# First blocks of a fused convolution, SiLU and product kernel: new list, two rounding steps on VectorE, seven products of zeros ahead of the first block's products

## The chip, the cores and the metric

The kernel runs on one core of a Trainium2 chip. The metric is the device time of one execution in microseconds (us). Five engines work in it, each on its own instruction stream and in the order of that stream: TensorE (PE, matrix products; PEld is its weight load), VectorE (DVE), ScalarE (ACT), GpSimd (POOL) and SyncE (SP), which here only issues DMA transfers. An engine waits at an instruction whose input is not ready, and everything behind that instruction on the same engine waits with it.

## The reference

The input `x` is 8 sequences of 4096 tokens with 192 channels. Each channel is convolved along its sequence with 7 causal taps, which the 24 channels of a head share and which are a softmax of `weight`. The result goes through `h = x @ w_in` (192 to 2048), `g = h * sigmoid(h)`, and `g @ w_out` (2048 to 192).

```python
w = np.exp(weight - np.max(weight, axis=-1, keepdims=True))
w = w / (np.sum(w, axis=-1, keepdims=True) + 1e-09)
...
out = np.einsum('hk,bskhg->bshg', w, x_unf)
...
h = x @ w_in
g = h * (1.0 / (1.0 + np.exp(-h)))
return (g @ w_out).astype(np.float32)
```

`w_in` and `w_out` come as float64; the kernel reads them as pairs of 32-bit words and rounds them to float32 itself.

## The kernel before

The 32768 tokens are worked in 32 blocks of 1024. All arithmetic is float32. Block 0 goes a plain way (`up_plain` and `down_plain`: every product as the reference has it). Blocks 1 to 31 use a scheme of fast matrix multiplication, in which sums of inputs, of weights and of results replace part of the products; for that, sums of the rounded weights are formed once (`combine` and `combine_out`).

Ahead of the blocks stands a preamble, in the order of its lines: taps, the convolution of block 0, and the rounding of the weights. `rounded` (L460) turns 128x768 pairs of words into float32 by a row of VectorE instructions; one of them needs the exponent `ex` scaled, and line 484 does that on ScalarE. `round_in(j)` rounds a quarter of `w_in`, `round_out(q)` a quarter of `w_out`. The loop of L944 to L951 runs `up_plain(0, 0)`, `round_in(2)`, `up_plain(0, 1)`, `round_in(3)`, `up_plain(0, 2)`, `round_out(0)`, `up_plain(0, 3)`, `round_out(1)`; then follow `round_out(2)`, the transposes of block 1's input and its halo, and `round_out(3)`. `up_plain` ends each of its products with a SiLU on ScalarE, so that on ScalarE the scaling of a rounding stands behind the SiLUs of the `up_plain` before it. GpSimd forms the weight sums of groups 0 and 1 (`combine((0, 1), ...)`, L967) beside this.

From L972 the order of all engines is written out by hand. `START` is a string of 763 tokens for the first blocks, `PLAN` a string that is repeated for every later block. `step(2, t)` runs each token of `START`: a leading `=` means block 0 (for `v`, `sp`, `w`, `i`, `ha` and `ld`, which work for the block after: block 1), `-` means block 1 (for those six: block 2), no sign block 2 (for those: block 3) and `+` block 3. The tokens that the prediction speaks of:

- `ld.k` loads a third of a block's input (4 DMAs on SP); `i.k` transposes it (VectorE, L611); `ha.0` fetches the six tokens ahead of the block (a copy on ScalarE, two DMAs on SP).
- `v.ki` is tap i of the convolution of third k: tap 0 on ScalarE (L642), taps 1 to 6 on VectorE (L645). A block has 18 of them on VectorE.
- `sp.n` spreads the convolved thirds over the slots of `dup` and `win`: n = 0, 1, 2, 4, 6 and 10 by ScalarE (L664), n = 3, 5, 7, 8 and 9 by DMA on SP (L666).
- `w.i` (L674) forms sums of slots on VectorE: `w.0` needs `sp.4`, `sp.7`, `sp.8` and `sp.9`; `w.3` needs `sp.5`; `w.4` needs `sp.3`, `sp.6` and `w.3`; `w.5` needs `w.4`.
- `go.0` to `go.3` are the sums of the weights of groups 2 and 3 (`combine`, 7, 6, 8 and 7 VectorE instructions), `co.0` to `co.3` those of the output weights (`combine_out`, 7, 7, 7 and 4).
- `dp.0` to `dp.47` are block 0's plain products with the output weights (L809, 4 matmul instructions each); `cp.k`, `o.k` and `st.k` copy, transpose and store block 0's result.
- `Pr.g` is product r (0 to 19) of group g (0 to 3) of a block (L721; a float32 product is two matmul instructions). Operand slot and half of the array's rows come from the table `PRODUCT`: `P7` reads the slot that `w.4` writes, `P1` that of `w.5`; products of the upper and of the lower row half can run beside each other when they are neighbours in the list. Block 1 has 80 of them.
- `u`, `j`, `k`, `h`, `i15_f`, `S` and so on are the steps between products (L755, L757, L768 on ScalarE, L746 and L771 on VectorE), `s` the sums of activations (L783), `Qr.q` the products with the output weights (L791).

`heat(times)` (L566) issues matmuls of zeros; the preamble calls it for 4 and 2 of them at its beginning.

Of the kernel before, what the change touches and what calls it, by code (L numbers as in the profile page):

```python
# [11 lines left out]
AF = mybir.ActivationFunctionType  # L12
ALU = mybir.AluOpType
# [4 lines left out]
def kernel(  # L18
# [19 lines left out]
    P = 128  # L38
# [20 lines left out]
    psum = ctx.enter_context(tc.tile_pool(name="ps", bufs=8, space=PSUM))  # L59


    PLAN = (
# [22 lines left out]
    )  # L85
    START = (
# [56 lines left out]
    )  # L143
    SPREAD = ((3, 0), (4, 1), (6, 0), (8, 1), (0, 1), (6, 1), (8, 0), (0, 0), (1, 0), (1, 1), (3, 1))
    PRODUCT = {0: (1, 9, 4, 'b1'),
# [164 lines left out]
    vec, act = Pinned(nc.vector), Pinned(nc.scalar)  # L310
# [4 lines left out]
    homes = {"bank": [], "up": []}  # L315
# [141 lines left out]
        for a in range(2):  # L457
            queue.dma_start(out=raw[:, a, :, :], in_=out32[a, q])

    def rounded(dst, words, shared):  # L460

        lo, hi = words[:, :, :, 0], words[:, :, :, 1]
        x_, y_ = dst.shape[1:]
# [8 lines left out]
        one = 1 << 20  # L472
# [8 lines left out]
            act.sign(st, st)  # L481
        else:
            vec.tensor_single_scalar(st, st, 1, op=ALU.min)
        act.activation(ex, ex, AF.Copy, bias=-float(896 * 8 * one), scale=8.0)
        vec.tensor_scalar(
            mh, hi, scalar1=one - 1, scalar2=one, op0=ALU.bitwise_and, op1=ALU.bitwise_or
        )
# [16 lines left out]
    def round_in(j, k=None):  # L504

        words = raws["i", j].rearrange(AS[j], a=2, k=NK)
        words = words.rearrange("p a k (c t) -> p a k c t", t=2)
        if k is None:
            rounded(
                wr[j].rearrange("p a k c -> p a (k c)"),  # L510
                words.rearrange("p a k c t -> p a (k c) t"),
                j < 2,
            )
        else:
            rounded(wr[j][:, :, k, :], words[:, :, k], j < 2)
        if k in (None, NK - 1):

            del raws["i", j]
            for e in range(2):
                nc.gpsimd.dma_start(  # L520
                    out=ws[j][R * e : R * e + R], in_=wr[j][R - R * e : 2 * R - R * e]
                )

    def round_out(q):
        rounded(
            wd[:, q, 0:12, :].rearrange("p (a s) d -> p a (s d)", a=2),
            raws.pop(("o", q)).rearrange("p (a x t) -> p a x t", a=2, t=2),
            q >= NJ // 2,
        )

    def comb(out, u, v, op):
# [31 lines left out]
    load_in(0, nc.sync, (0,))  # L563


    def heat(times):  # L566
        for _ in range(times):
            pin(
                nc.tensor.matmul(  # L569
                    idle[:, 0 : 2 * P],  # L570
                    zeros,
                    zeros.unsqueeze(1).to_broadcast([P, 2, P]),
                    start=True,
                    stop=True,
                )
            )
# [395 lines left out]
    homes["bank"].extend(bank() for _ in range(8))  # L972
    homes["up"].extend(u_all[:, i, :] for i in range(10))
    downs = down_plain(0)
    for t in START.split():
        step(2, t)
    for b in range(3, NB + 2):
        for s in plan:
# [32 lines left out]
```

## Time and profile before

| | |
|---|---|
| median of three runs | 2317.04 us (2316.29 to 2317.12) |
| the profiled execution, its own time | 2317.84 us |
| span from first to last instruction in it | 2316.1 us |
| mean granted TensorE clock | 0.993 |
| TensorE busy | 2294.7 us, 99% |
| VectorE busy | 2126.6 us, 92% |
| ScalarE busy | 1505.7 us, 65% |
| GpSimd busy | 234.2 us, 10% |

In the views that follow, a row of a timeline gives the start, the time to the end of the merged group, the engine, the line, the instruction, output and inputs, the shape and the count. In brackets stands how long the engine was idle ahead of it, and which instruction released it. `L308` is the line of a helper that many instructions go through, so its rows are told apart by their tiles. A row of windows gives, for one stretch of time, the busy time and the instruction count of each engine, then the granted TensorE clock as a share of full speed, the DMA share and GB/s.

### The profile page before, as it was taken

To read this page: it belongs to the slowest core of one execution; us is meant where nothing else is said; L and a number is where in the kernel's file an instruction comes from. 1 tells how busy PE (TensorE), PEld (TensorE's weight loads), DVE (VectorE), ACT (ScalarE), POOL (GpSimd) and SP (SyncE) were. 2 spreads that over 40 slices of the span, in tenths; PEclk is the share of its full clock that TensorE was granted. 3 is DMA by queue.
4 is the path that set the end of the run, shared out by engine and by line. 5 is a ranking of instruction groups with operands and counts; after the bars stand their busy time and mean duration, and the time that the engine had idled before them with its cause. 6 is when DMAs were issued, how large, how long until landed. Compare 5 with 4: busy or idle time off the path is not lost.

```text
span 2316.1 us, 40531 instructions
## 1 busy us (share of the span) xinstructions
PE 2294.7 (99%) x15334; PEld 1375.0 (59%) x15334; DVE 2126.6 (92%) x3137; ACT 1505.7 (65%) x2960; POOL 234.2 (10%) x301
## 2 busy tenths in 40 slices
PE   9899999999999999999999999999999999999998
PEld 5245666656566556566566666566665565665665
DVE  7989999999999999999999999999999999999976
ACT  5266666776666766667766667766667766677653
POOL 3300111000110000110001110001100001100011
PEclk9899999999999999999999999999999999999999
DMA  7214455334554334554335553345543345543345
GB/s 173 35 30 78 90 103 100 67 71 73 103 104 86 69 70 85 103 103 76 71 69 95 103 101 69 70 71 103 103 88 70 69 84 103 103 76 70 72 79 92
DMA packets 465525, 195.73 MB, mean 85 GB/s; under 512 B 422000, under 2 KB 427120, under 8 KB 465328
## 3 DMA queue, kind: packets, MB, share of 16 engines
q0 software_dynamic: 31696, 115.36, 26.8%
q1 hardware_dynamic: 429440, 77.25, 19.1%
q8 instruction: 120, 1.97, 0.3%
q10 hardware_dynamic: 4192, 0.52, 0.2%
q14 instruction: 77, 0.63, 0.1%
HBM read 31.46 MB, written 25.17 MB: 24 GB/s over the span
## 4 chain that ended last, share of the span: by engine, by line
PE 97%; DVE 2%; DMA 1%; issue 0%; ACT 0%; DVEq 0%; SPq 0%; POOLq 0%; ACTq 0%
PE ps L721 48%; PE ps L791 46%; PE ps L699 2%; DVE u L308 1%; PE ps L906 1%; DVE nat L645 1%; DMA g<-g 0%; PE ps L809 0%; PE ps L569 0%; DVE xt L611 0%; DVE w_other L308 0%; DMA dup<-nat 0%; DVE w_own L308 0%; DVE wd L308 0%; DVE dup L674 0%
## 5 line engine op out<-in xcount | busy, mean ns | idle before, releaser
L791 PE MATMUL ps<-g,wd 128*64 128x256 f32 x9920 | 1091.5, 380 | 0.2
L791 PEld LDWEIGHTS ps<-g,wd 128*64 128x64 f32 x9920 | 703.7, 137 | 415.9 <-issue 25.8
L783 DVE TENSOR_TENSOR g<-g 128x1024 f32<-128x1024 f32 x589 | 702.0, 1219 | 21.8 <-PE ps L791 7.9
L721 PE MATMUL ps<-win,w_own 64*128 64x512 f32 x1488 | 663.6, 602 | 9.3 <-DVE win L674 7.6
L721 PE MATMUL ps<-dup,w_other 64*128 64x512 f32 x1240 | 515.2, 599 | 0.9 <-ACT ps L757 0.8
L721 PE MATMUL ps<-dup,w_own 64*128 64x512 f32 x1240 | 484.7, 595 | 0.0
L721 PE MATMUL ps<-win,w_other 64*128 64x512 f32 x992 | 478.0, 600 | 0.0
L645 DVE SCALAR_TENSOR_TENSOR nat<-xt,turned,nat 128x512 f32<-128x512 f32 x558 | 399.5, 746 | 0.5 <-ACT nat L642 0.4
L757 ACT ACTIVATE ps<-ps 128x512 f32<-128x512 f32 (+1 forms) x465 | 254.7, 548 | 206.5 <-PE ps L791 176.2
L768 ACT ACTIVATE g<-ps 128x512 f32<-128x512 f32 x620 | 363.9, 603 | 22.2 <-DVE g L771 10.6
L721 PEld LDWEIGHTS ps<-win,w_own 64*128 64x128 f32 x1488 | 253.9, 187 | 152.9 <-issue 69.5
L771 DVE TENSOR_TENSOR g<-g,ps 128x512 f32<-128x512 f32 x496 | 331.4, 681 | 13.7 <-PE ps L721 10.1
L771 DVE TENSOR_TENSOR ps<-u,ps 128x512 f32<-128x512 f32 x372 | 254.4, 692 | 36.5 <-PE ps L721 19.6
L721 PEld LDWEIGHTS ps<-dup,w_own 64*128 64x128 f32 x1240 | 201.7, 186 | 141.8 <-issue 45.6
L777 POOL DMA_DIRECT2D g<-g x217 | 187.8, 910 | 952.5 <-DVE g L783 372.7
L721 PEld LDWEIGHTS ps<-dup,w_other 64*128 64x128 f32 x1240 | 190.7, 186 | 75.0 <-ACT ps L757 43.8
L755 ACT COPY u<-ps 128x512 f32<-128x512 f32 x341 | 200.2, 588 | 52.1 <-PE ps L721 48.4
L721 PEld LDWEIGHTS ps<-win,w_other 64*128 64x128 f32 x992 | 179.9, 188 | 86.7 <-issue 69.2
L768 ACT ACTIVATE g<-g 128x512 f32<-128x512 f32 x372 | 210.8, 624 | 3.1 <-DVE g L771 1.6
L757 ACT ACTIVATE fin<-ps 128x256 f32<-128x256 f32 x93 | 35.6, 383 | 211.4 <-PE ps L791 211.4
L771 DVE TENSOR_TENSOR fin<-fin,ps 128x256 f32<-128x256 f32 x248 | 94.3, 410 | 85.2 <-PE ps L791 83.4
L755 ACT COPY ps<-ps 128x512 f32<-128x512 f32 (+1 forms) x217 | 120.3, 555 | 66.9 <-PE ps L791 57.0
(92 smaller groups left out, 1166.5 us busy)
## 6 DMA issues: line engine op xcount, KB each, us to landing
g<-g POOLq DMA_DIRECT2D x217, 512.0 KB, 5.3
nat<-in_x_dram SPq DMA_DIRECT2D x382, 64.0 KB, 3.4
out_dram<-fin SPq DMA_DIRECT2D x244, 96.0 KB, 4.9
dup<-nat SPq DMA_DIRECT2D x97, 128.0 KB, 2.3
win<-nat SPq DMA_DIRECT2D x62, 128.0 KB, 2.3
fin<-in_moe_w_in_dram SPq DMA_DIRECT2D x8, 192.0 KB, 5.0
w_other<-w_own POOLq DMA_DIRECT2D x8, 192.0 KB, 6.5
g<-in_moe_w_out_dram SPq DMA_DIRECT2D x4, 384.0 KB, 6.7
```

The lines of the kernel that those rows point to most:

```text
L308: return lambda *args, **kw: pin(getattr(self.engine, name)(*args, **kw))
L645: nc.vector.scalar_tensor_tensor(out=dst, in0=src, scalar=tap, in1=dst, op0=ALU.mult, op1=ALU.add)
L699: nc.tensor.matmul(hs[a, n, e], rows(wr[j], e)[:, a, k, :], rows(d, e)[:, n, k, :], start=k == 0, stop=k == NK - 1,)
L721: nc.tensor.matmul(at(b, "bank", to, g), raw(g, w, e), rows(slot_of(b, x_), e), start=first, stop=True, skip_group_check=True,)
L755: pin(nc.scalar.copy(seen[to], seen[u]))
L757: pin(nc.scalar.activation(seen[to], seen[u], AF.Copy, scale=-1.0))
L768: pin(nc.scalar.activation(seen[to], seen[u], AF.Silu, scale=float(sign)))
L771: pin(nc.vector.tensor_tensor(seen[to], seen[u], seen[v], op=op))
L777: nc.gpsimd.dma_start(out=flat(g_all[:, q, to]), in_=flat(g_all[:, q, u + v - to]), accum_op=ALU.add)
L783: pin(nc.vector.tensor_tensor(to, u, v, op=ALU.add if sign > 0 else ALU.subtract))
L791: nc.tensor.matmul(acc[R * h : R * h + R, 0:HT], wd[:, 2 * q + e, w, :], g_all[:, q, slot, e, ts(h, HT)], start=False, stop=True, skip_gro ...
L906: nc.tensor.matmul(by_pe[k][n], rows(diag, n)[:, k, i, :], rows(xts[0], n)[:, k, i : i + TB], start=i == 0, stop=i == K - 1,)
```

## The change

Three things are changed. `START` becomes another order of the same 763 tokens; `PLAN` stays. The exponent's scaling moves from ScalarE to VectorE in two of the rounding steps, `round_in(3)` and `round_out(0)`. And seven matmuls of zeros, 128x128 by 128x512, are issued into the last free PSUM bank directly ahead of the first `P` token of `START`.

```diff
+    HEAT = 7
...
     START = (
-        "=v.00 -ld.2 =v.20 =go.0 =v.01 =v.21 =v.10 =v.11 =v.22 -ld.0 =v.12 =v.02 -ld.1 =v.13 "
-        "=v.23 =v.14 =v.24 =v.15 =v.25 =v.03 =v.26 =v.04 =v.16 -i.2 =v.05 =sp.7 -i.1 =v.06 -i.0 "
-        "=go.1 =sp.4 =sp.0 =sp.8 =sp.9 =w.0 =sp.10 =w.1 -ha.0 =sp.5 =dp.0 =w.2 -v.10 =sp.3 -v.11 "
-        "-v.20 =sp.6 =sp.2 -v.21 =w.3 -v.22 =w.4 -v.23 =sp.1 =dp.1 -v.12 =w.5 -v.13 =go.2 =dp.2 "
-        "-v.14 =go.3 -v.24 =dp.3 =dp.4 =dp.5 -v.15 -v.00 =dp.6 =dp.7 -v.25 =co.0 -v.01 =dp.8 "
...
-        "=dp.33 =dp.34 =dp.35 =dp.36 =dp.37 =dp.38 =dp.39 =dp.40 =dp.41 =dp.42 =dp.43 =dp.44 "
-        "-P7.1 -P7.0 -h15.1 -P8.1 -h15.0 =dp.45 -P1.1 -u4.1 -k12.1 -P8.0 =dp.46 -h17.1 =cp.1 "
-        "=cp.0 -u4.0 -P5.0 -P1.0 -k12.0 -k8.0 -h17.0 -P5.1 -P2.0 -j4.0 =dp.47 =cp.2 -k8.1 -P2.1 "
...
+        "=v.00 =v.10 =v.01 =v.11 =v.02 =v.12 =v.20 =v.03 =v.13 =v.21 =v.04 =v.22 =v.14 =v.23 "
+        "=dp.0 =v.15 =v.24 =v.05 =v.25 -ld.2 =v.16 =v.26 =v.06 -ld.0 -i.2 -ld.1 =sp.4 -i.0 =sp.0 "
+        "=sp.2 -i.1 =sp.10 =sp.8 =sp.7 =co.0 =sp.9 =w.0 =w.1 -ha.0 -v.20 =dp.1 -v.21 =dp.2 =w.2 "
+        "=dp.3 -v.10 -v.22 =sp.5 =sp.3 =sp.1 =w.3 =sp.6 =dp.4 -v.11 =dp.5 =dp.6 -v.00 -v.01 =w.4 "
+        "-v.23 -v.12 =go.0 =dp.7 =w.5 =go.2 -v.24 =dp.8 =dp.9 =dp.10 =dp.11 =dp.12 =dp.13 =dp.14 "
+        "=dp.15 =dp.16 =dp.17 =go.1 -v.13 =dp.18 =go.3 =dp.19 =dp.20 =dp.21 =dp.22 =dp.23 =dp.24 "
+        "=dp.25 =dp.26 =dp.27 =dp.28 =dp.29 =dp.30 =dp.31 =dp.32 =dp.33 =dp.34 =dp.35 -v.02 "
+        "=dp.36 =dp.37 =dp.38 =dp.39 =dp.40 -P7.1 =dp.41 =dp.42 =dp.43 -P7.0 -P1.0 =dp.44 =dp.45 "
+        "-P1.1 -k12.1 -h17.1 -h15.1 =dp.46 =cp.0 -k12.0 -P17.1 -P8.1 -P2.0 -P18.1 -h15.0 -P8.0 "
+        "=cp.1 -u4.0 -h17.0 -P2.1 -P5.0 -P18.0 -j4.0 -u4.1 =dp.47 =cp.2 -P17.0 -k8.0 =o.1 -P5.1 "
+        "=co.1 -k5.0 -P11.0 -S19.0 -S19.1 -P16.0 -P3.0 -P6.0 -u6.0 -k8.1 -u10.0 -h18.0 -P9.0 "
...
-    def rounded(dst, words, shared):
+    def rounded(dst, words, shared, scaled_by_act=True):
...
-        act.activation(ex, ex, AF.Copy, bias=-float(896 * 8 * one), scale=8.0)
+        if scaled_by_act:
+            act.activation(ex, ex, AF.Copy, bias=-float(896 * 8 * one), scale=8.0)
+        else:
+            vec.tensor_scalar(
+                ex, ex, scalar1=float(896 * one), scalar2=8.0, op0=ALU.subtract, op1=ALU.mult
+            )
...
                 j < 2,
+                j < 3,
             )
...
             q >= NJ // 2,
+            q > 0,
         )
...
-    def heat(times):
+    def heat(times, into=None):
+        to = idle[:, 0 : 2 * P] if into is None else into
         for _ in range(times):
             pin(
                 nc.tensor.matmul(
-                    idle[:, 0 : 2 * P],
+                    to,
                     zeros,
-                    zeros.unsqueeze(1).to_broadcast([P, 2, P]),
+                    zeros.unsqueeze(1).to_broadcast([P, to.shape[1] // P, P]),
...
     downs = down_plain(0)
+    cold = True
     for t in START.split():
+        if cold and t.lstrip("-=+")[0] == "P":
+            cold = False
+            heat(HEAT, homes["bank"][-1])
         step(2, t)
```

Within the new list, the tokens of block 2 and 3 are reordered too: of block 2's convolution, `v.14` and `v.15` stand at the end of block 1's products and `v.16` among its `Q` tokens, where the list before has them early and at the end of the products. `dp.41` to `dp.44`, which stood ahead of `P7.1`, stand between `P7.1` and `P1.1`.

93 rows, old and new, of the table START are left out of this document.

## The prediction

> **What bounds the kernel now.** I read the page first (TensorE busy 99%), then the chain of waits (97% TensorE; behind 164 us it repeats a block's pattern with nothing between), so the change is worth what it does in the first 164 us. There I took TensorE's timeline:
>
> ```profile
> 93.73 4.89 PE L809 MATMUL ps<-g,wd 128*64 128x512 f32 x22
> 106.22 3.75 PE L721 MATMUL ps<-win,w_own 64*128 64x512 f32 x4 [7.60 <-DVE win L674]
> ...
> 118.97 1.12 PE L721 MATMUL ps<-win,w_own 64*128 64x512 f32 x2 [1.67 <-ACT u L755]
> ```
>
> TensorE works without a gap until 98.62, waits 7.60 us for `w.4`, and starts block 1's products at 106.22. Windows of 1 us show what follows from the wait:
>
> ```profile
> 103.00:104.00 1.00, 0.00 (x0) 0.00 (x0) 1.00 (x2) 0.97 (x2) 0.00 (x0) 0.66 0.10 16
> 116.00:117.00 1.00, 1.00 (x4) 0.00 (x0) 1.00 (x3) 0.78 (x2) 0.00 (x0) 0.51 0.00 0
> 117.00:118.00 1.00, 0.30 (x2) 0.00 (x0) 1.00 (x3) 0.65 (x2) 0.00 (x0) 1.00 0.00 0
> 120.00:121.00 1.00, 1.00 (x3) 0.41 (x2) 1.00 (x3) 0.00 (x0) 0.00 (x0) 0.70 0.00 0
> 130.00:131.00 1.00, 1.00 (x6) 0.64 (x4) 1.00 (x3) 0.00 (x0) 0.00 (x0) 0.68 0.00 0
> ```
>
> The last but two number is the granted clock: it falls to half at 103.3, is full from 117.0 to 120.4, and half again until 130.6. [...] Who is late? VectorE, busy throughout:
>
> ```profile
> 41.10 0.96 DVE L308 SCALAR_TENSOR_TENSOR u<-fin,u 128x768 int32<-128x768 int32 x1 [1.89 <-ACT u L308]
> ...
> 51.40 1.32 DVE L308 SCALAR_TENSOR_TENSOR u<-u 128x768 int32<-128x768 int32 x1 [3.96 <-ACT u L308]
> ...
> 61.70 1.31 DVE L308 SCALAR_TENSOR_TENSOR u<-g,u 128x768 int32<-128x768 int32 x1
> ...
> 82.14 0.41 DVE L308 TENSOR_TENSOR w_other<-w_other 64x256 f32<-64x256 f32 x1
> ...
> 85.07 10.68 DVE L645 SCALAR_TENSOR_TENSOR nat<-xt,turned,nat 128x512 f32<-128x512 f32 x16
> ...
> 105.40 0.67 DVE L674 TENSOR_TENSOR win<-win 128x512 f32<-128x512 f32 x1
> ...
> 117.43 2.68 DVE L308 TENSOR_TENSOR wd<-wd 128x256 f32<-128x256 f32 x7
> ...
> 124.82 0.70 DVE L771 TENSOR_TENSOR ps<-u,ps 128x512 f32<-128x512 f32 x1 [2.78 <-PE ps L721]
> ```
>
> The rows are: the two scalings that come late from ScalarE, the same step in `round_out(1)`, `go.0`, the convolution, `w.4`, `co.0`, and `j4.0`, the first combination of products. ScalarE's rows tell why the scalings are late:
>
> ```profile
> 50.52 0.84 ACT L308 ACTIVATE u<-u 128x768 int32<-128x768 int32 x1
> ...
> 59.85 1.09 ACT L308 ACTIVATE g<-ps 128x512 f32<-128x512 f32 x2 [1.49 <-PE ps L699]
> 60.82 0.85 ACT L308 ACTIVATE u<-u 128x768 int32<-128x768 int32 x1
> ```
>
> Each stands behind the SiLUs of an `up_plain`, which TensorE paces.
>
> **What the stall costs now.** From 95.17 (the end of `dp.40`: 98.62 less 16 instructions of 38.84/180 = 0.216) to 163.81, where the `Q` run begins, 68.64 us pass. The work in it at steady rates: 28 `dp` instructions x 0.216 = 6.0, 160 `P` instructions x 31.43/144 = 34.9, 8 `Q` instructions x 30.37/280 = 0.9; 41.8 in all. Lost: 26.8 us.
>
> **Two roundings on VectorE.** Each adds one 128x768 tensor_scalar, 0.5 us by its neighbours (two in 1.03), and takes away a wait of 1.89 and of 3.96. `round_out(0)` then ends 4.8 us earlier, near 49.3 instead of 54.1. `round_out(1)` keeps its scaling on ScalarE, behind the last SiLU, which TensorE sets to 60.9, so VectorE stands from 57 to 61.7 and goes on at 61.70 as before. The gain moves one step on and is gone: 0. At best GpSimd's sums (46.5 to 77.6) end 1.4 us earlier, as `round_in(3)` frees them earlier; that would take up to 0.5 off `round_out(3)`, whose first rows at 75.80 take 1.55 instead of 1.03. I count 0; bounds 0 and 4.75.
>
> **The list, up to the first product.** I walk VectorE from 82.14. `go.0` (82.14 to 85.07) no longer stands first. 18 taps x 10.68/16 = 12.0: 94.15. Three transposes x 0.63: 96.05. `co.0`, 2.60: 98.65. It fills the wait for the spreading DMAs: `sp.8`, `sp.7` and `sp.9` are released when third 2 is done at 93.5, are issued until 95.3 (three took 1.78) and land 2.05 later. `w.0`, `w.1` x 0.60: 99.85. Tap 0.67, `w.2`, tap, `w.3` (102.4), two taps, `w.4`: 104.4. On SP the 12 loads of block 2 were issued from 77.35 on and hold nothing up; the two DMAs of `ha.0`, now ahead of `sp.5` and `sp.3`, wait for the transposes at 96.05, so these two are issued until 98.6 and land by 100.7, ahead of `w.3` at 101.8 by 1.1. `P7.1` starts at 104.5 instead of 106.22. Bounds: 101.1, the end of the zeros, and 106.2.
>
> **The zeros.** 14 instructions. The second preamble call ran 4 of 256 columns in 1.11, the last with its tail, 0.21 each; 512 columns double it: 0.427 x 14 = 5.97. They lie from 95.17 to 101.15, where TensorE would otherwise wait, so they delay nothing; without that cover they would cost 5.97. Idle left: 3.35 us. [...]
>
> [...]
>
> **From 104.5 to `j4.0`.** VectorE after `w.4`: two taps 1.33, `go.0` 2.93, `w.5` 0.60 (109.3: `P1.0` waits for it), `go.2` 3.29, tap, `go.1` 2.07, tap, `go.3` 2.69, tap: 119.4. There it reaches `j4.0`, 5.4 us before the 124.82 of now. TensorE with ScalarE (`k12.1`, `h17.1`, `h15.1`, `cp.0`, `k12.0`, `h15.0`, `cp.1`, `u4.0` at 0.5 to 0.6 each) has ten products and six `dp` done near 118.6, at full clock or with half until 110.17 within 0.4 us, because VectorE arrives no sooner. Work 20 x 0.218 + 24 x 0.216 = 9.6 in 14.1: 4.5 lost. Bounds: 2.1 (five products without a neighbour on the other row half) and 14 (all at half clock, 9.6 more).
>
> **From there to the `Q` run.** The chain `u4.0`, `j4.0`, `k5.0`, `co.1`, `k8.1`, `P11.1` leaves TensorE waiting near 120 and 123, 1.6 us by the rows. In the rest both engines are near full; the rows of before lose 2.6 there (29.6 us from 134.21 to 163.81 for 120 `P` and 8 `Q` instructions, 27.0). Sum 4.2; bounds 2.6 and 8.
>
> **The sum.** Lost now 26.8; lost then 5.97 + 3.35 + 4.5 + 4.2 = 18.0. Gain 8.8 us, on the profiled execution's 2317.84 (span 2316.1 and 1.7 around it): 2309.0. The median of the runs shown lies 0.8 lower, so 2317.0 - 8.8 = 2308.2. From 155 us on TensorE's work is the same as now. ScalarE loses two instructions off the path.
>
> **Rivals.**
> [...] 14%.
> The rounding gain comes through: VectorE starts the convolution 4.75 us earlier, `w.4` is ready at 99.7, the zeros end last and the 3.35 us of idle vanish; with the earlier `j4.0` gain near 13, 2304. Against it: the ScalarE row at 60.82. 6%.
> The order moves the wait only: `go.0` to `go.3` behind `w.4` hold `w.5` and `j4.0` up to their old times; gain under 2, 2316. Against it: VectorE's rows after 98 leave 8.6 us idle from 122 to 137, time that the work can move into. 4%.
> [...] 8%.
>
> **How the numbers follow.** The forecast has 68%, its own range is 2305 to 2311.5. A change of 0.2% is 4.6 us, about what a measurement of this kernel can tell. Faster by more: the forecast, the rounding case and a third of the half-clock case, 0.78. Within: the rest of that and the moved wait, 0.14. Slower: 0.08. The range 2304.5 to 2314.5 takes in the half-clock case and leaves out the slow one and the far ends.
>
> **What would show it.** Right: VectorE waits for ScalarE once near 57 to 61.7 and no longer at 41 and 51; zeros from 95.2 to 101.1; `P7.1` near 104.5; full clock from 110.2 on; `j4.0` near 119.4; the `Q` run near 155. Wrong: VectorE past 61.7 early, half clock after 111, a TensorE wait of over 1 us near block 2's first products.

## The result

The changed kernel takes 2310.89 us (median of 9 runs, 2310.26 to 2311.85) against 2317.12 us before (also 9 runs, 2316.29 to 2318.36). The ratio is 0.9975, with a 95% interval of 0.9965 to 0.9984: 6.2 us less. Its profiled execution has a span of 2309.5 us, 6.6 less than before. TensorE's timeline of the changed kernel answers to the one shown ahead (the line numbers of later code are 9 higher, so L721 is L730 and L791 is L800; in e2, e3 and e11 below they are 7 higher):

```profile
95.25 6.28 PE L578 MATMUL ps<-zeros 128*128 128x512 f32 x14
103.74 1.15 PE L730 MATMUL ps<-win,w_own 64*128 64x512 f32 x2 [2.21 <-DVE win L683]
104.82 4.39 PE L818 MATMUL ps<-g,wd 128*64 128x512 f32 x12
...
118.83 1.61 PE L730 MATMUL ps<-win,w_own 64*128 64x512 f32 x4 [0.68 <-ACT u L764]
...
155.17 20.08 PE L800 MATMUL ps<-g,wd 128*64 128x256 f32 x184
```

The zeros run where TensorE waited, the first product starts at 103.74 instead of 106.22, and the run of `Q` instructions begins at 155.17 instead of 163.81. VectorE's timeline shows the rounding, the convolution, `w.4` and `j4.0`:

```profile
55.61 1.37 DVE L309 SCALAR_TENSOR_TENSOR u<-u 128x768 f32<-128x768 int32 x1
61.85 1.24 DVE L309 SCALAR_TENSOR_TENSOR u<-g,u 128x768 int32<-128x768 int32 x1 [4.88 <-ACT u L309]
...
81.57 12.01 DVE L654 SCALAR_TENSOR_TENSOR nat<-xt,turned,nat 128x512 f32<-128x512 f32 x18
...
102.92 0.67 DVE L683 TENSOR_TENSOR win<-win 128x512 f32<-128x512 f32 x1
...
118.81 0.69 DVE L780 TENSOR_TENSOR ps<-u,ps 128x512 f32<-128x512 f32 x1 [0.20 <-ACT u L764]
```

The two old waits are gone and one of 4.88 us stands at `round_out(1)`. The granted clock in windows of 1 us (the last but two number):

```profile
104.00:105.00 1.00, 1.00 (x4) 0.19 (x5) 1.00 (x3) 0.00 (x0) 0.00 (x0) 0.83 0.00 0
107.00:108.00 1.00, 1.00 (x4) 0.24 (x2) 1.00 (x3) 0.00 (x0) 0.00 (x0) 0.50 0.00 0
108.00:109.00 1.00, 1.00 (x6) 0.14 (x2) 0.94 (x3) 0.00 (x0) 0.00 (x0) 0.97 0.00 0
```

It is half from 104.65 to 108.07, for 3.4 us, where before it was half for 23.9 of the 27.3 us from 103.3 to 130.6.

So 8.64 us are gained by the `Q` run, and the span ends 6.64 ahead. Where do 2 us go? Call the time by which an instruction of TensorE starts earlier than the one of the same number before its lead. It is 8.64 through block 1's `Q` run, 8.44 until block 3's first products, and 6.99 soon after. TensorE's timeline there, and GpSimd's, which issues the sums of activations that go by DMA:

```profile
258.13 2.81 PE L800 MATMUL ps<-g,wd 128*64 128x256 f32 x24
262.10 1.08 PE L800 MATMUL ps<-g,wd 128*64 128x256 f32 x8 [1.16 <-DMA g<-g]
```

```profile
244.75 2.64 POOL L786 DMA_DIRECT2D g<-g  x3 [6.00 <-PE ps L800]
257.46 0.86 POOL L786 DMA_DIRECT2D g<-g  x1 [10.07 <-DVE fin L775]
```

The row at 257.46 is block 2's `s11.1`. The three at 244.75 are block 2's `s5.0`, `s0.1` and `s5.1`, in this order. They land at 249.37, 251.97 and 256.93. `s11.1`, which adds to the slot that `s5.1` writes, is issued 0.53 us after that last landing and lands at 262.06; `Q4.1` starts at 262.10. The releaser named in its row is another one, but in e3, e4 and e6 to e10 too `s11.1` is issued 0.52 to 0.54 us after `s5.1` has landed. Before the change GpSimd issued block 2's `s5.1` ahead of `s5.0`, then `s11.1` ahead of `s0.1`, and TensorE did not wait (`Q` instructions at the same place):

```profile
254.91 1.75 POOL L777 DMA_DIRECT2D g<-g  x2 [6.81 <-PE ps L791]
260.47 1.75 POOL L777 DMA_DIRECT2D g<-g  x2 [3.81 <-DVE dup L674]
```

```profile
266.56 3.67 PE L791 MATMUL ps<-g,wd 128*64 128x256 f32 x32
```

Another 0.4 us are lost behind the last product; every run below with the new list shows that, none with the old, and its cause stays open.

### The profile page after: what moved, and what is told of

Its sections match the earlier page's. It is cut to its first block, busy times and chain, and to the rows that moved or that the text cites. A ratio compares the mean times of both kernels' runs of the same rounds, so it can differ in the third digit from the quotient of the medians.

```text
span 2309.5 us, 40541 instructions
## 1 busy us (share of the span) xinstructions
PE 2293.7 (99%) x15348; PEld 1375.8 (60%) x15348; DVE 2125.3 (92%) x3139; ACT 1504.2 (65%) x2958; POOL 234.6 (10%) x301
## 4 chain that ended last, share of the span: by engine, by line
PE 97%; DVE 2%; DMA 1%; issue 0%; ACT 0%; DVEq 0%; POOLq 0%; ACTq 0%
PE ps L730 48%; PE ps L800 46%; PE ps L708 2%; DMA g<-g 1%; DVE u L309 1%; DVE nat L654 1%; PE ps L915 1%; PE ps L818 0%; PE ps L578 0%; DVE wd L309 0%; DVE xt L620 0%; DVE fin L775 0%; DVE win L683 0%; DVE dup L683 0%; DVE fin L780 0%
## 5 line engine op out<-in xcount | busy, mean ns | idle before, releaser
L800 PE MATMUL ps<-g,wd 128*64 128x256 f32 x9920 | 1091.5, 380 | 1.4 <-DMA g<-g 1.2
L800 PEld LDWEIGHTS ps<-g,wd 128*64 128x64 f32 x9920 | 703.7, 137 | 417.1 <-issue 25.8
L730 PE MATMUL ps<-win,w_own 64*128 64x512 f32 x1488 | 657.3, 598 | 2.9 <-DVE win L683 2.2
L730 PE MATMUL ps<-dup,w_other 64*128 64x512 f32 x1240 | 513.1, 598 | 0.0
L730 PE MATMUL ps<-dup,w_own 64*128 64x512 f32 x1240 | 486.5, 595 | 0.0
L730 PE MATMUL ps<-win,w_other 64*128 64x512 f32 x992 | 475.2, 596 | 0.3 <-ACT g L764 0.3
L780 DVE TENSOR_TENSOR g<-g,ps 128x512 f32<-128x512 f32 x496 | 330.1, 677 | 11.8 <-PE ps L730 8.2
L730 PEld LDWEIGHTS ps<-win,w_own 64*128 64x128 f32 x1488 | 251.4, 186 | 144.3 <-issue 57.4
L730 PEld LDWEIGHTS ps<-dup,w_own 64*128 64x128 f32 x1240 | 202.6, 186 | 141.0 <-issue 56.3
L780 DVE TENSOR_TENSOR ps<-u,ps 128x512 f32<-128x512 f32 x372 | 253.4, 689 | 31.9 <-PE ps L730 16.2
L730 PEld LDWEIGHTS ps<-dup,w_other 64*128 64x128 f32 x1240 | 189.7, 185 | 71.7 <-ACT ps L766 42.5
L730 PEld LDWEIGHTS ps<-win,w_other 64*128 64x128 f32 x992 | 179.8, 186 | 85.1 <-issue 65.0
L780 DVE TENSOR_TENSOR fin<-fin,ps 128x256 f32<-128x256 f32 x248 | 93.8, 407 | 87.4 <-PE ps L800 85.9
```

The costliest lines, as they stand in the source:

```text
L730: nc.tensor.matmul(at(b, "bank", to, g), raw(g, w, e), rows(slot_of(b, x_), e), start=first, stop=True, skip_group_check=True,)
L780: pin(nc.vector.tensor_tensor(seen[to], seen[u], seen[v], op=op))
L800: nc.tensor.matmul(acc[R * h : R * h + R, 0:HT], wd[:, 2 * q + e, w, :], g_all[:, q, slot, e, ts(h, HT)], start=False, stop=True, skip_gro ...
```

## The experiments

One table for all, from each run's trace (start of block 1's first and eleventh product, of the 41st `Q` instruction, of the 21st product instruction of block 3; then the time at half clock from 90 to 136 us) and the medians. Traces are of one execution each, and their clock differs from execution to execution. The runs of before beside the experiments have medians of 2317.44 to 2318.05; one of these 52 runs took 2312.03, the others 2315.9 to 2319.5.

| run | first | eleventh | `Q` | block 3 | half clock | span | median (range) |
|---|---|---|---|---|---|---|---|
| before | 106.22 | 127.63 | 167.31 | 272.85 | 23.9 | 2316.1 | 2317.12 (2316.3 to 2318.4) |
| changed | 103.74 | 118.83 | 158.68 | 265.79 | 3.4 | 2309.5 | 2310.89 (2310.3 to 2311.9) |
| e1, roundings alone | 105.84 | 127.49 | 166.17 | 271.60 | 23.9 | 2315.0 | 2317.45 (2316.2 to 2318.5) |
| e2, zeros alone | 107.10 | 126.68 | 164.87 | 270.74 | 13.7 | 2314.5 | 2316.25 (2308.4 to 2318.0) |
| e3, list alone | 104.30 | 120.80 | 160.64 | 266.51 | 10.2 | 2310.2 | 2312.59 (2311.9 to 2314.2) |
| e4, changed, no zeros | 103.73 | 120.42 | 160.26 | 266.00 | 10.2 | 2310.1 | 2310.97 (2310.8 to 2312.1) |
| e5, old list, three roundings | 103.42 | 124.39 | 162.58 | 267.95 | 17.1 | 2311.6 | 2313.95 (2308.3 to 2316.2) |
| e6, changed, order of sums | 103.40 | 120.16 | 160.00 | 266.46 | 6.8 | 2309.5 | 2309.64 (2309.4 to 2311.2) |
| e7, changed, third rounding, four zeros | 101.65 | 116.74 | 156.58 | 262.32 | 3.4 | 2306.5 | 2307.87 (2306.9 to 2308.2) |
| e8, changed, ten zeros | 103.81 | 117.72 | 157.56 | 264.27 | 0 | 2307.4 | 2309.09 (2308.8 to 2309.2) |
| e9, third rounding and order | 102.20 | 116.25 | 156.09 | 261.83 | 0 | 2306.0 | 2307.58 (2307.2 to 2307.8) |
| e10, ten zeros and order | 103.81 | 117.75 | 157.59 | 263.60 | 0 | 2307.1 | 2308.59 (2308.6 to 2308.8) |
| e11, old list, nine zeros | 106.39 | 121.76 | 160.90 | 266.67 | 6.8 | 2310.0 | 2311.90 (2308.5 to 2313.9) |

**e1: the two roundings alone.** The old `START`, no zeros, both new arguments.

```diff
+                j < 3,
...
+            q > 0,
```

> The kernel before with only the two rounding steps on VectorE. Theory (the gain moves one step on): VectorE loses its waits at 41 and 51 us, and waits some 4.9 us for ScalarE in round_out(1), going on at 61.8; w.4 within 0.6 us of its old 106.1; time within 1 us of before, 2316.1 to 2317.5. Rival (the gain comes through): w.4 near 101.5 us, an idle of TensorE of 3 us instead of 7.6, and 2310 to 2313 us.

VectorE's and TensorE's timelines of this run:

```profile
61.83 1.50 DVE L309 SCALAR_TENSOR_TENSOR u<-g,u 128x768 int32<-128x768 int32 x1 [4.61 <-ACT u L309]
```

```profile
105.84 3.75 PE L730 MATMUL ps<-win,w_own 64*128 64x512 f32 x4 [7.08 <-DVE win L683]
```

The gain moved one step on, as the first theory has it: ratio 0.9999 (0.9990 to 1.0008). Block 1's first product starts 0.4 us earlier than before, and nothing of that is left in the median.

**e2: the zeros alone.** Old list, old roundings, `HEAT = 7`.

> The kernel before with only the seven products of zeros. Zeros from 98.6 to 104.6 us, first product still at 106.2, idle left 1.6 us. [...] Theory B (the zeros are worth nothing, since VectorE sets the pace): within 1 us of before, 2316 to 2318.

Theory B does not hold as written. The runs fall apart: seven between 2316.1 and 2318.0 with a mean granted clock of 0.995 or 0.996, four between 2308.4 and 2311.6 with 0.997 to 0.999. The profiled one is of the seven, TensorE and then the clock:

```profile
99.41 6.28 PE L576 MATMUL ps<-zeros 128*128 128x512 f32 x14
107.10 1.95 PE L728 MATMUL ps<-win,w_own 64*128 64x512 f32 x4 [1.41 <-DVE win L681]
```

```profile
109.00:110.00 1.00, 0.91 (x3) 0.29 (x2) 0.96 (x2) 0.60 (x1) 0.00 (x0) 0.78 0.05 8
110.00:111.00 1.00, 1.00 (x3) 0.29 (x4) 0.96 (x3) 0.20 (x1) 0.00 (x0) 0.50 0.05 16
```

The clock falls at 109.56 and is full again at 116.4. TensorE was idle for 1.41 us ahead of 107.10; from there to the fall it ran `P7.1`, `P7.0` and the beginning of `P8.1`, which all use the same half of the array's rows. Why the clock fell in this execution is not shown, nor that it makes the spread: only one of these runs has a trace, but the granted clocks of the others go with their times.

**e3: the list alone.**

> The kernel before with only the new list. [...] Rival (the zeros carry it): half clock to 120 us or later, time over 2314.

The rival fails: half clock ends at 110.5 and the time is 2312.59. The first product starts at 104.30, after 9.10 us of idle, at half clock from 100.3 to 110.5; three `dp` in a row run from 106.28 to 111.17. Most of the change's gain is here: 5.0 us against the runs of before beside it (2317.59), where the changed kernel without its zeros (e4) gains 6.6 against the same runs.

**e4: the changed kernel without the zeros.** `HEAT = 0`.

> The changed kernel without the seven products of zeros. Theory (half clock comes with or without them, and the three dp behind P7.1 end it): TensorE idle 95.2 to 103.7, half clock from about 101 to 108 or 111, j4.0 at 118.8 to 120; time 0 to 1.5 us over the changed kernel's 2310.9. Rival (the zeros keep the clock up): half clock past 115 us, 2314 or more.

In time the zeros are worth nothing, 2310.97 against 2310.89. The trace is less simple: TensorE's and VectorE's timelines show

```profile
103.73 2.04 PE L730 MATMUL ps<-win,w_own 64*128 64x512 f32 x2 [8.63 <-DVE win L683]
```

```profile
120.40 0.70 DVE L780 TENSOR_TENSOR ps<-u,ps 128x512 f32<-128x512 f32 x1 [1.80 <-ACT u L764]
```

With half clock from 100.1 to 110.4, `j4.0` comes 1.6 us later and so does the `Q` run (7.05 us ahead of before, not 8.64). But here nothing waits at block 3's first products (lead 6.84, and 6.78 soon after). In the profiled executions the zeros gain 1.6 us, and the wait for `s11.1` (1.16 us) and what follows it take 1.45 back.

e4 differs from e3 by the two roundings alone, and is 1.6 us faster by the medians (2310.97 against 2312.59). So with the new list the roundings are worth something, where e1 shows nothing with the old. The traces show 0.57 us of it at the first product and 0.4 at the `Q` run; the two profiled executions differ by only 0.13 us, and where the rest comes from is open.

**e5: old list, and a third rounding.** As e1, with `round_out(1)` on VectorE too.

```diff
-            q > 0,
+            q > 1,
```

> The kernel before (old list, no zeros) with the scaling of round_in(3), round_out(0) and also round_out(1) on VectorE. Theory (the wait for ScalarE moves on to the next rounding that still uses it behind an up_plain, and round_out(1) is the last of these): no wait of VectorE for ScalarE after 41 us, convolution 4 to 4.5 us earlier than the 84.7 of the run with two, first product near 101.5, idle of TensorE near 3 us; time 2309 to 2313. Rival (the roundings don't matter, or round_out(2) takes the wait over): first product within 1 us of 105.8, 2316 or more.

The wait is gone, but the gain is about half of what was expected: the convolution starts at 82.28 instead of 84.68 in e1 (2.4 us, not 4 to 4.5), the first product 1.9 us past the expected 101.5. Time 2313.95, ratio 0.9984 (0.9976 to 0.9993), spread 7.8 us. e7 shows why.

**e6: one sum moved.**

```diff
-        "Di15_f.0 sp.3 Q5.0 w.3 s0.1 w.4 w.5 ...
-        "s5.1 Du9.0 Dh16.0 ...
+        "Di15_f.0 sp.3 Q5.0 w.3 s5.1 s0.1 w.4 w.5 ...
+        "Du9.0 Dh16.0 ...
```

> The changed kernel with one token moved: block 2's s5.1 ahead of s0.1, so that it is the second and not the third of the three sums by DMA that are issued together at 244.8 us. Theory (s11.1 is issued only when s5.1 has landed, and Q4.1 waits for s11.1): s5.1 lands near 252, s11.1 near 257 to 260, no wait at Q4.1, and the gain of block 2 (8.4 us) holds at block 3's first products instead of 7.0; time 1.2 to 1.5 us under the changed kernel's, near 2309.5. Rival (the wait moves to Q17.1, which needs s0.1, or the loss has another cause): gain at block 3 of 7.0, 2310.9.

`s11.1` is issued at 254.56 instead of 257.46, and none of block 3's first products waits. The lead at block 3 is the one of block 2, 6.39 (6.33 soon after). It isn't 8.4: 1.3 us are lost because the clock in this execution was half for 6.8 us (103.4 to 110.2) instead of 3.4, and 0.7 us at block 2's entry (189.1 to 190.4), where by the trace a weight load waited for a VectorE instruction (L780). Time 2309.64, 1.25 us under the changed kernel, as expected; three of the five runs lie between 2309.4 and 2309.6, two at 2311.0 and 2311.2. e10 shows the same at full clock.

**e7: the changed kernel, third rounding, four zeros.**

```diff
-    HEAT = 7
+    HEAT = 4
...
-            q > 0,
+            q > 1,
```

> The changed kernel with round_out(1) scaled on VectorE too, and four products of zeros instead of seven (3.4 us, from 95.3 to 98.8). Theory (VectorE sets the pace from 57 us to the end of block 1's products): convolution from 77.3, w.4 near 99.3, first product 99.5, Q run 4 us earlier than 155.2, near 151; time 2306 to 2307.5. Rival (the Q run is bound by products, or block 2 and 3 give the 4 us back): 2309 or more.

The time is in the middle, 2307.87, and the `Q` run 2.1 us earlier, not 4. VectorE's timeline of `round_in(3)`, `round_out(1)` and the convolution:

```profile
37.44 0.94 DVE L309 SCALAR_TENSOR_TENSOR u<-fin,u 128x768 int32<-128x768 int32 x1
...
55.24 1.48 DVE L309 SCALAR_TENSOR_TENSOR u<-g,u 128x768 int32<-128x768 int32 x1
56.75 1.36 DVE L309 SCALAR_TENSOR_TENSOR u<-u 128x768 f32<-128x768 int32 x1
58.04 1.48 DVE L309 SCALAR_TENSOR_TENSOR u<-g,u 128x768 int32<-128x768 int32 x1
...
79.47 2.73 DVE L654 SCALAR_TENSOR_TENSOR nat<-xt,turned,nat 128x512 f32<-128x512 f32 x4
```

The same form of instruction took 0.94 at 37 us, before GpSimd's weight sums began, and takes 1.48 beside them. In the changed kernel GpSimd did a good part of those sums during VectorE's wait of 4.88 us, where each took 0.71 to 0.86 us; beside VectorE they take up to 1.45. From GpSimd's timeline in the changed kernel:

```profile
60.85 0.73 POOL L309 TENSOR_TENSOR w_own<-w_own 64x256 f32<-64x256 f32 x1
```

Without the wait the two run side by side until 76.4. The convolution starts at 79.47 instead of 81.57.

**e8: ten zeros.** `HEAT = 10` in the changed kernel.

> The changed kernel with ten products of zeros instead of seven, which close the idle ahead of the first product (95.2 to 103.9). Theory (half clock from 104.7 to 108.1 is hidden behind VectorE, w.5 at 108.3): full clock throughout, first product within 0.3 us of 103.7, j4.0 within 0.3 us of 118.8, time within 0.5 us of 2310.9. Rival (the half clock costs): j4.0 over 1 us earlier, 2309.5 or less.

The rival is right in the time and in that half clock costs; `j4.0` itself starts only 0.64 us earlier. The zeros end as the first product begins:

```profile
95.02 8.85 PE L578 MATMUL ps<-zeros 128*128 128x512 f32 x20
103.81 1.12 PE L730 MATMUL ps<-win,w_own 64*128 64x512 f32 x2
104.86 2.79 PE L818 MATMUL ps<-g,wd 128*64 128x512 f32 x12
...
260.57 1.08 PE L800 MATMUL ps<-g,wd 128*64 128x256 f32 x8 [0.54 <-DMA g<-g]
```

Full clock from 94 to 136 us. `j4.0` starts at 118.17, and VectorE no longer waits ahead of it (0.20 us in the changed kernel) or behind it (0.48); the eleventh product is 1.1 us earlier than with 3.4 us of half clock (the changed kernel), 2.4 us earlier than with 6.8 (e6) and 2.7 than with 10.2 (e4). Time 2309.09, and all five runs within 0.4 us. The last line is the wait for `s11.1` again.

**e9: third rounding, seven zeros, and the order.** e6 with `q > 1`.

> The changed kernel with round_out(1) scaled on VectorE too, its seven zeros kept, and block 2's s5.1 ahead of s0.1. Theory (zeros until 101.5 close the idle ahead of a first product at 101.7, so the clock stays full; the order keeps the gain at block 3): full clock from 95 us on, Q run near 155 to 156, gain of 10.5 to 11.5 us at block 3's first products; time 2305.5 to 2307, under the 2307.9 of the run with four zeros. Rival (four zeros were enough, one half-clock stretch costs nothing): 2307.9.

Full clock from 98 to 132 us, the lead of 11.02 us kept across block 3, 2307.58 us: ratio to before 0.9954 (0.9940 to 0.9969). It is the fastest of all and 3.3 us under the changed kernel, though 0.6 above the expected range. Against e7 the 0.3 us is within the spread of either.

**e10: ten zeros and the order.** e6 with `HEAT = 10`.

> The changed kernel with ten products of zeros and block 2's s5.1 ahead of s0.1. Theory (with the clock steady the order alone differs from the run with ten zeros, which waited 0.54 us for a sum by DMA at block 3's entry): no such wait, gain of 9.3 us kept at block 3; time 0.5 to 1 us under 2309.1, near 2308.4. Rival (the order makes no difference): 2309.1.

At the same clock the order alone takes away the 0.54 us wait (lead 9.24 on both sides, where e8 falls from 9.34 to 8.58) and 0.5 us of time.

**e11: old list, nine zeros.** e2 with `HEAT = 9`.

> The kernel before with nine products of zeros, which close the whole idle ahead of its first product (98.6 to 106.4). [...] Rival (only idle time lets the clock fall): full clock in all runs, 2308 to 2310, spread under 2 us.

The rival fails: 2311.9, spread 5.4 us. In the profiled run the zeros close the idle, and the clock holds through the first products (from 106.39) and `dp.45` and `dp.46` among them. It falls at 116.84, behind this wait of TensorE and 2.70 us of products that all use one half of the rows:

```profile
114.14 1.12 PE L728 MATMUL ps<-win,w_own 64*128 64x512 f32 x2 [1.73 <-ACT u L762]
```

Two of e11's six runs took 2308.5, with a mean granted clock of 0.999; two of e2's took 2308.4 and 2309.3 with the same. The new list at that clock takes 2309.09 with ten zeros (e8) and 2308.59 with the order of sums (e10), both with the two roundings. Where the clock stays full, the old list is thus as fast as the new one, some 9 us under before. In the traces without zeros the clock is half for 17.1 to 23.9 us with the old list (before, e1, e5) and for 10.2 with the new one (e3, e4); that the `dp` which the new list keeps back do this is the author's reading, not shown. These four runs of the old list have no trace; that their clock did not fall is read from the mean alone.

## Why the prediction was right, and where it was not

The forecast of 2308.2 us (own range 2305 to 2311.5) stands against 2310.89 measured: 6.2 us gained where 8.8 were forecast (6.6 between the two profiled executions).

- **The roundings, counted at 0.** With the old list shown by e1 and by the row at 61.85. The 0.5 us by GpSimd came in full: GpSimd's sums end 1.9 us earlier (75.7 instead of 77.6), and VectorE is free for the convolution at 81.57 where the walk began at 82.14. With the new list e4 and e3 differ by 1.6 us, more than these 0.57 explain. The other bound, 4.75, isn't to be had either: with the wait really gone (e5, e7) only 2.1 to 2.4 us come out.
- **The list up to the first product.** `P7.1` at 104.5 was forecast, 103.74 measured; the 0.57 of the convolution is most of the difference.
- **The zeros.** 5.97 us forecast, 6.28 measured with the tail of the last, idle left 2.21 instead of 3.35.
- **The clock.** Half clock came, from 104.65 to 108.07, and ended while the three `dp` ran (104.82 to 109.21). The 110.17 until which the prediction counts it was the author's estimate; no trace of the changed kernel shows it. That half clock costs no more than 0.4 us, "because VectorE arrives no sooner", was wrong: against e8 its 3.4 us cost 1.1 us, and half clock to 110 costs 2.4 (e6) to 2.7 us (e4). Under half clock it is `u4.0` on ScalarE, behind the late products, that `j4.0` waits for (1.80 us in e4). In e6, at half clock until 110.2, the 41st `Q` instruction comes 1.3 us later (160.00 instead of 158.68), so that the `Q` run met its forecast is in part luck.
- **`j4.0` and the `Q` run.** 119.4 and near 155 forecast, 118.81 and 155.17 measured: 8.64 us gained against 8.8.
- **"From 155 us on TensorE's work is the same as now".** This step failed. The work is the same, but 0.2 us are lost in block 2, 1.45 at block 3's first products and 0.4 at the end: 2.0 of the 2.2 us by which the profiled execution misses the forecast gain. The walk covered VectorE, SP and ScalarE to 119 us and GpSimd's queue nowhere behind; the new list issues `s5.1` as the third of three sums, with `s11.1` and `Q4.1` hanging on it. e6 and e10 undo the 1.45 with one token.
- **The lost 26.8 us.** The sum did not separate half clock from the rest. By the runs of the old list at a mean clock of 0.999 (e2, e11), some 9 us of them go with half clock, an estimate; at that clock the new list is no faster than the old one with zeros. So the change gains by less half clock (3.4 us instead of 23.9 in the two traces).
- **The rivals.** Half clock past 111 did not come, nor a slower kernel. Block 2's `w.4` has no wait in it; the loss sat one wait further, in the DMA sums of the same stage.

## What to carry to other kernels

When a wait is removed from an engine, look for the next instruction on it that takes something from the same late producer: here, with the old list, the whole gain stood there. Then ask who used the wait: here GpSimd, whose sums took 0.71 to 0.86 us each while VectorE stood still and up to 1.45 beside it, and beside which a VectorE instruction took 1.48 us instead of 0.94 (e7). And when a list is reordered, check every queue for chains (a transfer that waits for a transfer), since being early by 8 us is worth only what the last of such a chain lets through. And before a new order is credited with a gain, compare it with the old one at the same granted clock.

## What the runs showed of the hardware

- The granted clock fell behind waits of different length, and also while TensorE worked. Before the change it fell at 103.3, within the wait of 7.60 us (98.62 to 106.22). In the changed kernel it fell at 104.65, behind a wait of 2.21 us (until 103.74); in e2 at 109.56, behind one of 1.41 us (until 107.10); in e11 at 116.84, behind one of 1.73 us (until 114.14). What decides it is not shown.
- Half clock also ended in different ways. In the changed kernel it ended after 3.4 us (108.07), with `P7.1` and `dp.41` to `dp.43` running in it. In e2 it lasted 6.8 us (109.56 to 116.4), with `dp` and products of one row half mixed. In the trace of before TensorE was at work again from 106.22 and full clock came at 117.0. What brings it back is open.
- The same list met half clock at different times. The changed kernel and e6 run the same list up to block 2 and start block 1's first product at 103.74 and 103.40, but the clock fell at 104.65 in one and at 103.35 in the other; the times of e2, e5 and e11 spread over 5 to 10 us, while those of e8, e9 and e10, whose profiled executions show full clock there, spread over 0.2 to 0.6.
- In the changed kernel `s5.1` was as late as its slowest part. It lands in 16 parts; 14 of them had landed by 254.50 us and the last at 256.93. A transfer of the queue of kind "instruction", 16,384 bytes, began at 254.70 and took 1.07 us. That the one held the other up is not shown.
- VectorE beside GpSimd: in e7 a scalar_tensor_tensor of 128x768 took 0.94 us at 37.44, before GpSimd's 64x256 sums began, and 1.48 at 55.24, beside them.
